# Reordering the first two batches of an attention-plus-MoE kernel, and unused matmuls in its pauses

## The chip, the cores and the metric

The kernel runs on one core of a Trainium2 chip. The core has a matrix engine (TensorE: PE in the profile, PEld for its weight loads), a vector engine (VectorE, DVE), a scalar engine (ScalarE, ACT), a general engine (GpSimd, POOL), and SyncE (SP), which here only issues DMAs. Each engine works through its own queue in order and waits on semaphores that the others raise. The metric is device microseconds of one execution; lower is better.

## What is computed

The attention takes 8 batches of 8 heads, 576 queries each, 64 numbers a head, and 16 extra "beacon" keys and values that every query may see. Its output, laid out as 4608 tokens of 512 numbers, goes through two matrices with a leaky ReLU between them.

```python
k_all = np.concatenate([beacon_k, k], axis=2)      # 16 + 576 keys
v_all = np.concatenate([beacon_v, v], axis=2)
scores = q @ k_all^T / 8                           # causal over the 576, beacons open
a = exp(scores - max); a /= sum(a)
attn = a @ v_all                                   # (8, 8, 576, 64)
x = attn.transpose(0, 2, 1, 3).reshape(4608, 512)
h = x @ w_in                                       # 512 -> 2048
out = max(0.01 * h, h) @ w_out                     # 2048 -> 512
```

## The kernel before

**Groups.** A group g is one batch and one pair of heads: 8 x 4 = 32 groups. The keys, beacons first, form five blocks of at most 128 (c = 0 to 4). Scores are computed with keys on the partitions and queries along the row, so the causal shape makes later blocks narrower. `score(g, n)`, n = 0 to 3, does the matmuls of one PSUM tile of two banks (L297), each as two matmuls on 64 partitions for the two heads, and the exponential into SBUF (L306, ACT). Two such PSUM tiles exist, so score n waits for the exponential n-2. `masks(g)` zeroes what a query may not see, with four affine_selects on POOL (L320). There are three buffers of probabilities, used in turn.

**From probabilities to x.** `value(g, half)` multiplies probabilities by values, which carry a column of ones so that the sums come along (L351: 12 matmuls in half 0, 18 in half 1), then takes reciprocals (L360) and scales (L361) on DVE. `x_transposes(g)` turns the result with five transposes (L373) and copies it to xT (L378). `finish(g)` does that and notes how many chunks of 512 tokens are ready for the two MoE matrices.

**MoE work as filling.** `fill()` emits one piece of MoE work: either `moe1` (four 128x512 matmuls, L387, and a Prelu on ACT, L394) or a quarter of `moe2` (four matmuls, L409; after the fourth quarter a copy by DVE, L418, and a store by SP). The total number of pieces is fixed. From group 8 on, what is left is spread over the steps of a group by the slots of the main loop; after the last group the rest is done in a row.

**Two ways of turning q and k.** For batches 0 and 1 (groups 0 to 7), `t_q(g, which)` turns them on TensorE: 18 transposes of 64x64 (L247) and a copy from PSUM (L250). For k a small copy of the turned beacon keys into kT comes first (L238). From batch 2 on the data are permuted on POOL (`permute`, L164), turned by DMA (`turn_pairs`, L262) and put in order on POOL (`in_order`, L275 and L277), one group ahead of its scores. kT has two buffers.

**Loads.** q and k of batches are loaded by POOL's queue, with a cast on the way (`load_qk`, L135, four DMAs for half a batch); the very first pair of heads comes uncast by SP's and ACT's queues (`load_first_pair`, L152) and is cast by DVE (q, L471) and ACT (k, L472). Values come by SP's queue (`load_v`, L210 to L215) and are cast by POOL (`cast_v`, L224, one instruction for each key block). The MoE weights come by POOL's queue (L109, L114), in groups 3 to 6. Before the first scores, 34 matmuls of the identity with itself are issued whose result nobody reads (`warm_up`, L444), and the beacon keys of batch 0 are turned (`beacon_transposes`, L186, with copies L191).

**Order.** The order of every queue is written out by hand: the order of the statements in the source is that of each engine's queue. In the loop over groups, `loads(g)` comes first (POOL and SP), then for g < 8 scores 0 and 1, `finish(g-3)`, the transposes for the next group, `value(g-2, 0)`, scores 2 and 3, `value(g-2, 1)`, and the masks. At g = 8 a block without scores finishes groups 5 to 7 with fills between and then does 22 fills, while POOL and the DMAs bring batch 2.

Of the kernel before, what the change touches and what calls it, by code (L numbers as in the profile page):

```python
# [8 lines left out]
FP32 = mybir.dt.float32  # L9
# [6 lines left out]
def kernel(  # L16
# [11 lines left out]
    nc = tc.nc  # L28
# [64 lines left out]
    def make_ones():  # L93
        for t in v_bufs:
            nc.gpsimd.memset(t[:, :, :, D : D + 1], 1.0)
# [83 lines left out]
            in_=bk_raw[:, b0:b1, None, :].to_broadcast([128, b1 - b0, 2, D]),  # L179
        )  # L180

    def beacon_transposes(b0, b1):

        ps = ps_one.tile([128, 1024], BF16, name="tp", tag="one")
        for b in range(b0, b1):
            nc.tensor.transpose(  # L186
                ps[:, b * 128 : (b + 1) * 128], bk[:, b].rearrange("p e d -> p (e d)"), ident
            )
        for par in range(2):
            ps_ = slice(par * 64, par * 64 + 64)  # L190
            nc.vector.tensor_copy(  # L191
                out=bkT[ps_, b0:b1].rearrange("p b h n -> p (b h) n"),
                in_=ps[ps_, b0 * 128 : b1 * 128].rearrange("p (x e n) -> p e x n", e=2, n=NB)[:, par],
            )
# [26 lines left out]
    def cast_v(b, eng, c0=0, c1=NKB):  # L221
        t, dst = v_raws[b], v_bufs[b % 2]
        for c in range(c0, c1):
            eng.tensor_copy(out=dst[0 : ROWS[c], c, :, 0:D], in_=t[0 : ROWS[c], c])  # L224
# [61 lines left out]
    def score(g, n):  # L286
        qT, kT = qk[g]
        if n == 0:
            probs[g] = a_bufs[g % 3]
        aT = probs[g]  # L290
        parts = SCORES[n]
        sc = ps_sc.tile([128, 2, 512], FP32, name="sc", tag="sc")
        c0 = parts[0][3]
        for c, q0, w, col in parts:
            for par in range(2):
                ps_ = slice(par * 64, par * 64 + 64)
                nc.tensor.matmul(  # L297
                    out=sc[:, par, col - c0 : col - c0 + w],
                    lhsT=kT[ps_, c * 128 : (c + 1) * 128],
                    rhs=qT[ps_, q0 : q0 + w],  # L300
                    start=True,
                    stop=True,
                    skip_group_check=True,
                )
        w = sum(p[2] for p in parts)
        nc.scalar.activation(  # L306
            out=aT[:, :, c0 : c0 + w], in_=sc[:, :, 0:w], func=AF.Exp, scale=0.125
        )

    def masks(g):  # L310

# [125 lines left out]
            turn[0] = 0  # L437
        return can1 or can2

    def warm_up(n):  # L440

        ps = ps_one.tile([128, 512], FP32, name="av", tag="one")
        for i in range(n):
            nc.tensor.matmul(out=ps[:, 0:128], lhsT=ident, rhs=ident, start=True, stop=True)  # L444

    NG = B * NPAIR

    def has(g):
        return 0 <= g < NG
# [10 lines left out]
    with order:  # L460
# [5 lines left out]
        load_v(0, after=first)  # L466
        load_v(1)
        make_pads()
        make_ones()
        cast_beacon_k(0, 1, nc.scalar.copy)  # L470
        nc.vector.tensor_copy(out=first_cast[0], in_=first_raw[0])  # L471
        nc.scalar.copy(out=first_cast[1], in_=first_raw[1])  # L472
        cast_beacon_k(1, B, nc.gpsimd.tensor_copy)
        cast_v(0, nc.gpsimd, 0, 1)
        load_qk(1, 0)
        cast_v(0, nc.gpsimd, 1, 3)
        warm_up(34)
        beacon_transposes(0, 1)
        t_q(0, 0)
        t_q(0, 1, nc.scalar.copy)  # L480

        def loads(g):
            b, hp = divmod(g, NPAIR)
            if g == 1:
                cast_v(0, nc.gpsimd, 3, 5)
            elif g == 2:
                load_qk(1, 1)
            elif g == 3:
                cast_v(1, nc.gpsimd, 0, 3)
                load_w_in(0)  # L490
            elif g == 4:
                cast_v(1, nc.gpsimd, 3, 5)
                load_w_in(1)
                load_w_in(2)
            elif g == 5:
                load_w_in(3)
                load_w_out(0)
                load_w_out(1)
            elif g == 6:
                load_w_out(2)  # L500
                load_w_out(3)
            elif g == 7:
                load_qk(2, 0)
            elif g >= 2 * NPAIR:
                if has(g + 1):
                    in_order(g + 1)
                if b < B - 1:
                    if hp == 0:
                        load_v(b + 1)
                        load_qk(b + 1, 0)  # L510
                    else:
                        if hp < 3:
                            for which in range(2):
                                permute(b + 1, hp - 1, which)
                        if hp == 1:
                            load_qk(b + 1, 1)
                        else:
                            turn_pairs(b + 1, hp - 2)
                    if hp == 3:
                        cast_v(b + 1, nc.gpsimd)  # L520
# [5 lines left out]
        def finish(g):  # L526

            x_transposes(g)
            ready[0] = chunks_with(g)
            if g % NPAIR == NPAIR - 1:  # L530
                turn[0] = 1


        for g in range(NG + 3):
# [3 lines left out]
            if g < 2 * NPAIR:  # L538

                score(g, 0)  # L540
                score(g, 1)
                if has(g - 3):
                    finish(g - 3)
                if g == 2:
                    beacon_transposes(1, B)
                if g + 1 < 2 * NPAIR:
                    t_q(g + 1, 0)
                    t_q(g + 1, 1, nc.scalar.copy if g in (4, 6) else nc.vector.tensor_copy)
                if g > 2:
                    value(g - 2, 0)  # L550
                if g == 7:
                    fill()
                score(g, 2)
                score(g, 3)
                if g == 2:
                    value(0, 0)
                if g >= 6:
                    fill()
                if has(g - 2):
                    value(g - 2, 1)  # L560
                masks(g)
                continue

            if g == 2 * NPAIR:

                load_qk(2, 1)
                for grp in range(2):
                    for which in range(2):
                        permute(2, grp, which)
                    turn_pairs(2, grp)  # L570
                load_v(2)
                in_order(g)
                cast_v(2, nc.gpsimd)
                finish(g - 3)
                value(g - 2, 0)
                fill()
                value(g - 2, 1)
                fill()
                finish(g - 2)
                value(g - 1, 0)  # L580
                fill()
                value(g - 1, 1)
                fill()
                fill()
                finish(g - 1)
                for n in range(22):
                    fill()
                loads(g)
# [70 lines left out]
```

The softmax here doesn't subtract the row's maximum and nothing guards it: scores larger than these inputs give would overflow.

## Time and profile before

| | |
|---|---|
| median of 6 runs | 356.26 us (355.72 to 356.88) |
| the profiled execution | 357.3 us, its span 355.6 us |
| mean granted TensorE clock | 0.966 |
| PE busy | 341.3 us, 96% of the span |
| POOL busy | 202.4 us, 57% |
| ACT busy | 189.2 us, 53% |
| DVE busy | 95.3 us, 27% |
| DMA | 40.87 MB, mean 115 GB/s |

The span runs from the first to the last instruction on the core. Lines of the page give busy tenths for 40 equal slices of the span (8.9 us each); `PEclk` is the clock that TensorE was granted, in tenths of full speed. Lines of the timeline read: start in us, length in us, engine, source line, operation, output<-inputs, shapes, number of instructions merged, and in brackets the engine's idle time before and what ended it. An issue of a DMA by POOL counts as busy time of POOL.

### The profile page before, as it was taken

How to read it: one execution, taken by the hardware profiler on the slowest of the kernel's cores; microseconds unless marked ns; L12 is line 12 of the kernel's file. 1: busy time of each engine (PE TensorE's matmuls, PEld its weight loads, DVE VectorE, ACT ScalarE, POOL GpSimd, SP SyncE). 2: the span in 40 equal slices, each digit the busy share in tenths (PEclk: the TensorE clock that was granted, in tenths of full speed). 3: DMA queues.
4: the chain of work that ended last, by engine and by line, in shares of the span. 5: the costliest groups of instructions: out<-in, count | busy, mean ns of one | idle time of the engine just before them, and what ended most of it. 6: DMA issues, size and time to landing. Idle time of an engine off the chain costs nothing.

```text
span 355.6 us, 7297 instructions
## 1 busy us (share of the span) xinstructions
PE 341.3 (96%) x2959; PEld 175.2 (49%) x3002; DVE 95.3 (27%) x231; ACT 189.2 (53%) x278; POOL 202.4 (57%) x343
## 2 busy tenths in 40 slices
PE   5899999999999999999999999999999999999996
PEld 5567554434444444444444544444444554444444
DVE  2396550001434213311232223222322241000111
ACT  3947945387454873378337843686348403733300
POOL 7599847489898899957695769574441100000000
PEclk9556999999999999999999999999999999999999
DMA  8999999998897996992579355900110011000012
GB/s 166 212 207 161 195 207 198 225 181 135 125 200 131 160 171 103 152 230 41 97 139 223 65 98 107 184 2 1 61 59 2 0 62 59 2 29 29 31 59 88
DMA packets 86929, 40.87 MB, mean 115 GB/s; under 512 B 69872, under 2 KB 82160, under 8 KB 86896
## 3 DMA queue, kind: packets, MB, share of 16 engines
q1 hardware_dynamic: 73456, 26.75, 35.4%
q0 software_dynamic: 13152, 13.34, 25.0%
q8 instruction: 23, 0.38, 0.4%
q10 hardware_dynamic: 288, 0.33, 0.4%
q14 instruction: 10, 0.08, 0.1%
HBM read 37.22 MB, written 9.44 MB: 131 GB/s over the span
## 4 chain that ended last, share of the span: by engine, by line
PE 91%; DVE 3%; ACT 2%; DMA 1%; issue 1%
PE acc L409 35%; PE acc L387 35%; PE sc L297 9%; PE av L351 9%; PE tp L373 2%; PE tp L247 1%; DMA v_raw<-in_k_dram 1%; DVE osb L418 1%; ACT aT L306 1%; DVE xT L378 1%; DVE kT L238 1%; ACT k_cast L472 0%; PE tp L186 0%; DVE qT L250 0%; DVE kT L250 0%
## 5 line engine op out<-in xcount | busy, mean ns | idle before, releaser
L387 PE MATMUL acc<-xT,w_in_sb 128*128 128x512 bf16 x554 | 138.4, 379 | 2.7 <-DVE xT L378 1.4
L306 ACT ACTIVATE aT<-sc 128x1024 bf16<-128x1024 f32 (+3 forms) x128 | 104.3, 870 | 65.2 <-PE sc L297 65.0
L409 PE MATMUL acc<-w_out_sb,gT 128*128 128x512 bf16 (+1 forms) x571 | 136.3, 373 | 1.5 <-issue 0.6
L394 ACT ACTIVATE gT<-acc 128x512 bf16<-128x512 f32 x144 | 85.9, 601 | 79.2 <-PE acc L387 79.2
L320 POOL TENSOR_SCALAR_AFFINE_SELECT aT<-aT 128x384 bf16<-128x384 bf16 (+2 forms) x128 | 52.9, 447 | 52.5 <-PE av L351 40.0
L409 PEld LDWEIGHTS <-gT 128*128 128x128 bf16 x592 | 53.3, 98 | 58.7 <-issue 6.1
L387 PEld LDWEIGHTS <-w_in_sb 128*128 128x128 bf16 x576 | 51.9, 98 | 59.5 <-issue 4.2
L418 DVE COPY osb<-acc 128x512 f32<-128x512 f32 (+1 forms) x37 | 25.0, 677 | 134.7 <-PE acc L409 134.6
L351 PEld LDWEIGHTS <-aT 128*128 128x128 bf16 (+1 forms) x960 | 38.9, 101 | 14.9 <-issue 3.3
L351 PE MATMUL av<-v_aug,aT 128*128 128x65 bf16 (+1 forms) x960 | 42.2, 199 | 0.1
L297 PE MATMUL sc<-qT,kT 64*128 64x80 bf16 (+4 forms) x384 | 38.2, 305 | 3.0 <-ACT aT L306 1.5
L361 DVE TENSOR_TENSOR x_nat<-av,rec 128x384 bf16<-128x384 f32 x64 | 31.4, 491 | 2.2
L224 POOL CAST v_aug<-v_raw 128x512 bf16<-128x512 f32 (+1 forms) x40 | 23.2, 620 | 8.9 <-DMA v_raw<-in_v_dram 8.9
L277 POOL COPY kT<-k_turn 128x576 bf16<-128x576 bf16 x24 | 28.1, 1170 | 0.0
L277 POOL COPY qT<-q_turn 128x576 bf16<-128x576 bf16 x24 | 28.1, 1169 | 0.0
L360 DVE RECIPROCAL rec<-av 128x6 f32<-128x6 f32 x64 | 11.9, 186 | 59.9 <-PE av L351 59.9
L378 DVE COPY xT<-tp 128x576 bf16<-128x576 bf16 x32 | 14.5, 454 | 48.2 <-PE tp L373 48.2
L297 PEld LDWEIGHTS <-kT 64*128 64x128 bf16 x384 | 13.0, 97 | 28.7 <-issue 18.8
L135 POOL DMA_DIRECT2D k_raw<-in_k_dram x31 | 19.3, 624 | 2.9 <-DMA w_out_sb<-in_moe_w_out_dram 2.9
L135 POOL DMA_DIRECT2D q_raw<-in_q_dram x31 | 19.0, 613 | 2.0 <-DMA w_out_sb<-in_moe_w_out_dram 1.9
L164 POOL COPY q_nat<-q_raw 128x1152 bf16<-128x1152 bf16 x12 | 13.7, 1145 | 6.1 <-DMA q_raw<-in_q_dram 6.1
L373 PEld LDWEIGHTS <-x_nat 128*128 128x128 bf16 (+2 forms) x160 | 11.4, 100 | 9.6 <-DVE x_nat L361 2.0
(36 smaller groups left out, 89.7 us busy)
## 6 DMA issues: line engine op xcount, KB each, us to landing
out_dram<-osb SPq DMA_DIRECT2D x35, 256.0 KB, 2.0
v_raw<-in_v_dram SPq DMA_DIRECT2D x24, 256.0 KB, 5.2
q_raw<-in_q_dram POOLq DMA_DIRECT2D x31, 144.0 KB, 5.0
k_raw<-in_k_dram POOLq DMA_DIRECT2D x31, 144.0 KB, 5.5
w_in_sb<-in_moe_w_in_dram POOLq DMA_DIRECT2D x4, 512.0 KB, 6.8
w_out_sb<-in_moe_w_out_dram POOLq DMA_DIRECT2D x4, 512.0 KB, 12.0
v_raw<-in_v_dram SPq DMA_DIRECT2D x8, 224.0 KB, 3.9
v_raw<-in_v_dram SPq DMA_DIRECT2D x8, 160.0 KB, 5.0
```

The source lines that it names most:

```text
L135: dma = nc.gpsimd.dma_start(out=dst[e * RP : (e + 1) * RP], in_=src[b, h0 : h0 + 2].rearrange("h (p i) d -> p h i d", i=RI),)
L224: eng.tensor_copy(out=dst[0 : ROWS[c], c, :, 0:D], in_=t[0 : ROWS[c], c])
L277: nc.gpsimd.tensor_copy(out=dst.rearrange("c (p i) -> c p i", i=RI), in_=t[:, :, e].rearrange("c i p -> c p i"),)
L297: nc.tensor.matmul(out=sc[:, par, col - c0 : col - c0 + w], lhsT=kT[ps_, c * 128 : (c + 1) * 128], rhs=qT[ps_, q0 : q0 + w], start=True, s ...
L306: nc.scalar.activation(out=aT[:, :, c0 : c0 + w], in_=sc[:, :, 0:w], func=AF.Exp, scale=0.125)
L320: nc.gpsimd.affine_select(out=part, in_=part, compare_op=ALU.is_ge, fill=0.0, base=base, channel_multiplier=-1, pattern=pattern,)
L351: nc.tensor.matmul(out=avv[:, n, 0 : D + 1], lhsT=aT[0 : ROWS[c], par, a0 : a0 + 128], rhs=va[0 : ROWS[c], c, 2 * hp + par, :], start=(c = ...
L361: nc.vector.tensor_tensor(out=x_nat[:, t0:t1].rearrange("p t e d -> p (t e) d"), in0=avv[:, :, 0:D], in1=rec[:, n0:n1, None].to_broadcast( ...
L387: nc.tensor.matmul(out=acc, lhsT=w_in_sb[:, j, fc * 128 : (fc + 1) * 128], rhs=xT[:, j, i * 512 : (i + 1) * 512], start=(j == 0), stop=(j ...
L394: nc.scalar.activation(out=gT[i][:, fc, :], in_=acc, func=AF.Prelu, alpha=0.01)
L409: nc.tensor.matmul(out=acc[:, 0:w], lhsT=gT[i][:, fc, t * 128 : (t + 1) * 128], rhs=w_out_sb[:, fc, c0 : c0 + w], start=(fc == 0), stop=(f ...
L418: nc.vector.tensor_copy(out=osb[:, 0:w], in_=acc[:, 0:w])
```

## The change

Eight parts, all in the first two batches or ahead of them:

1. First keys: the cast of the first pair's k is split by head between ACT and DVE.
2. `warm_up(34)` becomes `keep_busy(34)`; five more runs of unused matmuls are put in: 6 after the first beacon transposes, 6 and 10 after the two first `t_q`, 12 at the end of group 0 and 6 at the end of group 1. All write one PSUM tile.
3. The copies of the first beacon keys go from DVE to ACT.
4. `make_ones` moves behind the cast of the remaining beacon keys on POOL; the value casts of batch 0 are all issued ahead of the loop: two blocks before `load_qk(1, 0)`, three behind it. Before, it was one, then two, and two more in group 1.
5. The masks of group 0 are made by DVE, by multiplying with a triangle of ones (`make_tri` on POOL, `masks_by_tri`).
6. In groups 0 to 7 the order becomes: scores 0 and 1, transposes for the next group, scores 2 and 3, both halves of `value(g-2)`, `finish(g-3)`.
7. The fills of groups 6 and 7 beside scores 2 and 3 go; one fill is added at g = 8, before `finish(5)`. One piece less is done before the 22 fills, and so one more later.
8. The beacon transposes of the other batches move from group 2 to group 1.

```diff
-    def beacon_transposes(b0, b1):
+    def beacon_transposes(b0, b1, copy=nc.vector.tensor_copy):
...
-            nc.vector.tensor_copy(
+            copy(
                 out=bkT[ps_, b0:b1].rearrange("p b h n -> p (b h) n"),
...
+    tri = singles.tile([128, 128], BF16, name="tri")
+
+    def make_tri():
+
+        nc.gpsimd.memset(tri, 1.0)
+        nc.gpsimd.affine_select(
+            out=tri,
+            in_=tri,
+            compare_op=ALU.is_ge,
+            fill=0.0,
+            base=0,
+            channel_multiplier=-1,
+            pattern=[[1, 128]],
+        )
+
+    def masks_by_tri(g):
+
+        aT = probs[g]
+        diag = aT[:, :, 512 : 512 + 3 * 464].rearrange("p e (c x) -> p e c x", c=3)[:, :, :, 0:128]
+        for part, seen in (
+            (aT[:, :, 0:112], tri[:, None, NB:128].to_broadcast([128, 2, 112])),
+            (diag, tri[:, None, None, :].to_broadcast([128, 2, 3, 128])),
+            (aT[0:80, :, 1648:1728], tri[0:80, None, 0:80].to_broadcast([80, 2, 80])),
+        ):
+            nc.vector.tensor_tensor(out=part, in0=part, in1=seen, op=ALU.mult)
...
-    def warm_up(n):
-
-        ps = ps_one.tile([128, 512], FP32, name="av", tag="one")
+    busy = []
+
+    def keep_busy(n):
+
+        if not busy:
+            busy.append(ps_one.tile([128, 512], FP32, name="av", tag="one"))
         for i in range(n):
-            nc.tensor.matmul(out=ps[:, 0:128], lhsT=ident, rhs=ident, start=True, stop=True)
+            nc.tensor.matmul(out=busy[0][:, 0:128], lhsT=ident, rhs=ident, start=True, stop=True)
...
-        make_ones()
         cast_beacon_k(0, 1, nc.scalar.copy)
         nc.vector.tensor_copy(out=first_cast[0], in_=first_raw[0])
-        nc.scalar.copy(out=first_cast[1], in_=first_raw[1])
+        keep_busy(34)
+        beacon_transposes(0, 1, nc.scalar.copy)
+        nc.scalar.copy(out=first_cast[1][:, 0], in_=first_raw[1][:, 0])
+        nc.vector.tensor_copy(out=first_cast[1][:, 1], in_=first_raw[1][:, 1])
+        make_tri()
         cast_beacon_k(1, B, nc.gpsimd.tensor_copy)
-        cast_v(0, nc.gpsimd, 0, 1)
+        make_ones()
+        cast_v(0, nc.gpsimd, 0, 2)
         load_qk(1, 0)
-        cast_v(0, nc.gpsimd, 1, 3)
-        warm_up(34)
-        beacon_transposes(0, 1)
+        cast_v(0, nc.gpsimd, 2, 5)
+        keep_busy(6)
         t_q(0, 0)
+        keep_busy(6)
         t_q(0, 1, nc.scalar.copy)
+        keep_busy(10)
...
-            if g == 1:
-                cast_v(0, nc.gpsimd, 3, 5)
-            elif g == 2:
+            if g == 2:
                 load_qk(1, 1)
...
                 score(g, 0)
                 score(g, 1)
-                if has(g - 3):
-                    finish(g - 3)
-                if g == 2:
-                    beacon_transposes(1, B)
                 if g + 1 < 2 * NPAIR:
                     t_q(g + 1, 0)
                     t_q(g + 1, 1, nc.scalar.copy if g in (4, 6) else nc.vector.tensor_copy)
-                if g > 2:
+                score(g, 2)
+                score(g, 3)
+                if g == 1:
+                    beacon_transposes(1, B)
+                if g < 2:
+                    keep_busy((12, 6)[g])
+                if g >= 2:
                     value(g - 2, 0)
+                    value(g - 2, 1)
+                if g >= 3:
+                    finish(g - 3)
                 if g == 7:
                     fill()
-                score(g, 2)
-                score(g, 3)
-                if g == 2:
-                    value(0, 0)
-                if g >= 6:
-                    fill()
-                if has(g - 2):
-                    value(g - 2, 1)
+                if g == 0:
+                    masks_by_tri(g)
+                    continue
                 masks(g)
                 continue
...
                 in_order(g)
                 cast_v(2, nc.gpsimd)
+                fill()
                 finish(g - 3)
                 value(g - 2, 0)
```

## The prediction

> **What bounds the kernel now.** I read the page first, then the windows of TensorE, the timeline, and last the POOL timeline further on.
>
> ```profile
> PE   5899999999999999999999999999999999999996
> PEclk9556999999999999999999999999999999999999
> 5.80:9.22 3.42, 1.57 (x46) 1.00 1.24 214
> 26.28:29.70 3.42, 3.42 (x62) 0.50 0.96 148
> 29.70:33.11 3.41, 3.41 (x42) 0.50 1.11 151
> 33.11:36.52 3.41, 3.03 (x82) 1.00 1.24 206
> ...
> 26.28:29.70 3.42, 1.75 (x41) 0.50 0.96 148
> 33.11:36.52 3.41, 0.95 (x40) 1.00 1.24 206
> ```
>
> The first two lines are the page's: TensorE is full in nearly every slice, so the time falls only by what makes it reach its dense part sooner. The clock row shows the opening at half clock: by the finer windows from 9.22 to 33.11. Windows read: busy, instructions, clock, DMA share, GB/s; the last two lines count transposes alone. The clock changes every 3.41 us at most. Take transposes off: 5.80:9.22 had only 0.52 us of other matmuls (its transposes took 1.05) and full clock was lost; 33.11:36.52 had 2.08 (3.03 - 0.95) and kept it; 26.28:29.70 had 1.67 and did not raise it; 29.70:33.11 had 3.13 and did. So transposes seem not to count.
>
> ```profile
> 9.02 3.16 ACT L306 ACTIVATE aT<-sc 128x1024 bf16<-128x1024 f32 x4 [0.49 <-PE sc L297]
> 21.51 0.99 PE L297 MATMUL sc<-qT,kT 64*128 64x512 bf16 x4 [0.66 <-DVE kT L250]
> 26.71 1.00 PE L297 MATMUL sc<-qT,kT 64*128 64x512 bf16 x4
> 36.68 0.43 PE L373 MATMUL tp<-ident,x_nat 112*128 112x112 bf16 x5
> 37.04 0.47 PE L247 MATMUL tp<-ident,q_raw 64*64 64x64 bf16 x18
> 37.73 0.54 PE L351 MATMUL av<-v_aug,aT 128*128 128x65 bf16 x12
> 38.21 0.48 PE L297 MATMUL sc<-qT,kT 64*128 64x336 bf16 x8
> 39.49 0.72 PE L351 MATMUL av<-v_aug,aT 128*128 128x65 bf16 x18
> ```
>
> Groups 3 and 4 begin at 21.51 and 26.71: 5.20 us a group at half clock, TensorE without a pause. At full clock the pieces are (start to start) x transposes 0.36, q and k transposes 0.69, values 0.48 and 0.66; four exponentials take ACT 3.16 (3.27 later).
>
> **Part by part: the start.** The first keys' cast, 1.15 us on ACT from 6.18, is halved between ACT (0.6) and DVE (0.94/2): keys' transposes start at 6.85, not 7.38, and the first score follows 1.21 later as now (7.38 to 8.59): 8.1. The 10 unused matmuls (0.053 each at full clock, half the 0.107 of the warm-up's 34) lie under that copy, the first 6+6 under the wait for the casts. Beacon copies moved to ACT (0.38 from 5.1) lie before the keys land at 6.16.
>
> **Groups 0 to 2, if the clock holds.** Group 0: first exponential 0.47 after its first score, two exponentials 1.86, so score 3 can go at 2.38 and ends at 2.55; 12 unused matmuls 0.64: group 1 at 8.1+3.2=11.3. The masks of group 0 go to DVE: three tensor_tensor of 224, 768 and 160 elements a partition, which the trace doesn't show. Below, at the rate of the 576-element copy in 0.46 (L378), 1152 elements: 0.9 us; above, by L361 (384 in 0.56, 256 in 0.42, so 0.14 each and 1.1 ns an element): 1.7. I take 1.3, as near to one as to the other; they wait for the fourth exponential (8.1+0.43+3.16=11.7) and push qT, kT of group 2 (0.76+0.16+0.75) to 14.8. Group 2 starts then, TensorE itself being free at 14.7 (7 beacon transposes 0.4 and 6 unused 0.32 included). Its values need batch 0's last rows, which land at 18.15 by the landing events; cast 0.6: they end near 18.95, however fast the rest is. This wait of 1.3 us covers the uncertain masks.
>
> DVE against POOL: the 128x16 copy (L238) takes 0.16 alone but 1.98 at 18.83, while POOL's masks run to 20.77. So the new masks may meet POOL's two casts at 12.5 to 14.2, 0.6 each, +1.2 at most; the cover takes that. [...]
>
> **Groups 3 to 7.** New order: scores, transposes, scores, both value halves, x transposes. Score 3 still waits 2.38 for the second exponential, then 0.17+0.48+0.66+0.36: 4.05 a group. That beats 5.20, but loses to the old order at full clock: there 35.84 to 44.19, 8.35 us, held two groups and three fills (0.87 each, from L387 to L409 to L387 at 58.82 and 59.68), 2.9 a group net, since values and fills lay in the wait for exponentials. Start of group 3 at 19.0, five groups 20.25, one fill: 40.1; then 3.94 (44.19 to 48.13 now) and the added fill 0.87: value(7,0) at 44.9 against 48.13. It has done one fill less: TensorE is ahead by 3.2-0.87=2.4 us. The fills find their weights: the last quarter of w_out is first read near 64.0-3.2 and lands at 52.00.
>
> Moves on POOL's queue: load_qk(1,0), four issues, now stands behind the second value cast, whose rows land at 13.54, so issues start near 14.1 instead of 13.06 and land near 19.0 to 22.1 (17.91 to 21.08 now). Group 3's transposes want the first at 19.5, k at 19.8: 0.3 lost, 1.05 at most. make_ones (1.06) goes into POOL's idle 3.62 before 12.51; make_tri likewise, after six issues; without that cover the first value cast would be 1.06 late. SP keeps its order. Masks 0 leave POOL (1.63), but its casts then wait for the rows of 18.15, so masks 1 start at 18.8 (19.18 now). Masks 4 to 7 (third piece done after 1.3, all after 1.6) follow two, three, two and four issues (0.75, the last four 0.6) from 29.44 on: third pieces done at 32.2, 36.1, 39.2 and 43.2; values 4, 5 and 7 want them at 33.7, 37.8 and 44.9, so nothing waits. One of the four single PSUM banks stays with the unused matmuls until group 1; three are left for two transposes a group, each copied out within 0.76: nothing.
>
> **What takes part of it back.**
>
> ```profile
> 28.63 1.16 POOL L224 CAST v_aug<-v_raw 128x512 bf16<-128x512 f32 x2
> 29.74 1.51 POOL L109 DMA_DIRECT2D w_in_sb<-in_moe_w_in_dram  x2
> ...
> 101.99 1.20 POOL L277 COPY kT<-k_turn 128x576 bf16<-128x576 bf16 x1
> 104.18 0.59 PE L297 MATMUL sc<-qT,kT 64*128 64x512 bf16 x4
> ```
>
> Group 13's kT is ready on POOL at 103.19 and used at 104.18: 0.99 to spare (groups 10 to 15: 3.86, 2.64, 1.08, 0.99, 1.33, 1.25). From 70 to 140 POOL is 87 to 99% busy, waiting for its own loads. What sets its start is not TensorE: batch 1's last values land at 28.69, only then are they cast (28.63 to 29.79) and the weight loads issued (29.74), DMA share stays near 1.2 until w_out lands at 52.00, and each load of batch 2 waits for one of these. I let this move up 0.3 (POOL's queue just before it is 0.3 to 0.5 earlier; bounds -0.5 and +1.2, the thin DMA stretch at 31.5 to 32.5). A 0.97 us wait of POOL for exponentials at 76.14 goes too, but the next q_nat (79.72) has its rows only at 79.58, so 0.14 counts. TensorE can keep 0.99+0.14+0.3=1.4 of its 2.4 us; the rest becomes waits for kT in groups 11 to 13. After that slack is 8 us and TensorE bounds to the end.
>
> Sum on the profiled execution: span 355.6-1.4=354.2, with its 1.7 around the span 355.9 against its 357.3; that execution lies 1.04 over the median of 356.26, so 354.9 in the runs' terms.
>
> **Does the clock hold?** In the same currency the windows of the new kernel would hold: first, 6 and 10 unused (0.5, 0.7 with their tails) and two scores 0.59: 1.8; second 0.48+0.83+0.59=1.9; third 1.6; then 2.33 per 4.05, 2.0. Known: lost at 0.52, kept at 2.08. They are nearer to the upper row, so I take held. [...]
>
> **Rivals.**
> - POOL's chain moves up with TensorE, whole: 2.4 kept, 353.9. For it, the waits for DMA in that chain; against, DMA saturated to 52 us.
> - The pieces cancel: batch 1's loads land a microsecond late and POOL's start slips 0.5: 355.6 to 356.9, no change.
> - Slower: the clock falls at 12.63 for want of counted matmuls. Group 1 takes 4.4 (six unused 0.64 and beacons 0.93 now on the path), group 2 4.7, groups 3 and 4 5.2, group 5 4.2 with the clock back: group 6 at 35.0, group 8 at 44.0, value(7,0) at 48.8, 0.65 behind and a fill short: +1.5, 357.8. It decides from about two lost groups (1.15 each against 2.4). For it, windows under 2.08; against, 0.52 lies far below.
>
> **Numbers.** Forecast 0.50, first rival 0.14, no change 0.09, slower 0.27. Under 0.2% (0.7 us) this kernel's measurement can't be told from no change. Forecast's own range 353.7 to 355.7 (POOL's bounds); the whole 353.4 to 358.0, leaving out the ends of the first and last case. Faster 0.58 (a little of the forecast falls inside 0.2%), same 0.12, slower 0.30.
>
> **What would show it.** Right: granted clock 1.00 from about 6 us, mean above 0.99; group 3 near 19, group 8's first fill near 40; waits of L297 for POOL's kT in groups 11 to 13. Wrong: half clock between 9 and 30 (third rival), kT waits absent with value(7,0) near 45 (first), q or k transposes waiting for DMA in group 3 (second).

## The result and the profile after

The median after is 359.27 us (27 runs, 356.63 to 362.76), the kernel before on the same chip 356.61 (62 runs, 355.04 to 359.65). The ratio is 1.0068, 95% interval 1.0052 to 1.0085: slower by 0.68%, where 354.9 was forecast, a gain of 1.4 on the 356.26 that was known then. Ratios, here and below, leave out slow executions, those over 1.5% above the fastest of their kernel (three of these 27), so they can differ from the quotient of two medians. The profiled execution took 357.61 us; only four of the 27 were quicker, so it flatters the kernel by 1.7 us.

From the page of the kernel after: span, TensorE's and POOL's busy tenths, the clock, and the queue kind "instruction" (packets, MB, share).

```profile
span 355.9 us, 7381 instructions
PE   8797899999899999999999999999999999999995
POOL 7499927399799599987695769574431100000000
PEclk9969999999999999999999999999999999999999
q8 instruction: 24, 0.39, 0.5%
```

The clock row shows one low slice where the kernel before had three, and TensorE's row begins with 8 where it had 5; the 7s and 8s behind it are the same work at a higher clock (mean granted 0.990 against 0.966). By these rows the opening is better, and the time must have gone elsewhere.

Windows of the kernel after, cut at the clock's own steps, which its trace shows at 5.35, 19.00 and 25.83, four and two times 3.41 us apart (busy us and instructions of PE, PEld, DVE, ACT, POOL, then clock, DMA share, GB/s); the last two lines count transposes and their copies alone (PE, DVE, ACT).

```profile
12.18:15.59 3.41, 2.77 (x77) 2.04 (x72) 2.37 (x6) 3.16 (x5) 1.61 (x3) 1.00 1.12 197
15.59:19.00 3.41, 2.02 (x58) 1.53 (x52) 1.92 (x5) 2.71 (x4) 3.41 (x7) 1.00 0.99 201
19.00:22.42 3.42, 3.29 (x59) 1.97 (x57) 1.95 (x5) 1.86 (x2) 3.42 (x8) 0.50 1.20 212
...
12.18:15.59 3.41, 1.38 (x59) 2.27 (x4) 0.00 (x0) 1.00 1.12 197
15.59:19.00 3.41, 0.41 (x27) 1.49 (x2) 0.00 (x0) 1.00 0.99 201
```

The clock fell at 19.00, behind the window with the least work (2.02 us), and stayed at half to 25.83. TensorE's timeline tells why that window is thin, and what it cost:

```profile
18.22 0.37 PE L377 MATMUL av<-v_aug,aT 128*128 128x65 bf16 x7 [0.52 <-POOL v_aug L224]
18.78 1.04 PE L377 MATMUL av<-v_aug,aT 128*128 128x65 bf16 x15 [0.18 <-POOL v_aug L224]
19.75 0.99 PE L297 MATMUL sc<-qT,kT 64*128 64x512 bf16 x4
...
25.01 0.97 PE L297 MATMUL sc<-qT,kT 64*128 64x512 bf16 x4
```

The values of group 0 wait for POOL's casts of batch 0's last rows, as the forecast had it; group 3, at half clock, then takes 5.26 us (19.75 to 25.01). At full clock the groups step by 3.93 (scores of groups 5, 6 and 7 at 29.14, 33.07, 37.00). Even so group 8 starts at 68.59 against 71.00: 2.4 us, less the piece of MoE work still owed (0.87), a lead of 1.5.

Where the lead goes is in the chain of waits of the kernel after (start, length, what):

```profile
85.34 1.60 POOL aT L346 x4
87.08 1.10 POOL qT L277
88.18 1.10 POOL kT L277
89.33 0.58 PE sc L297 x4
```

Before, this stretch of the chain is TensorE alone. Now it goes through POOL's masks and copies; scores of groups 11, 12 and 13 start 0.06 us after their kT. Group 13 starts at 104.22, before at 104.18. So much was forecast, with a loss of 1.0 of 2.4. What was not forecast is that POOL's chain itself is later: kT of group 9 is ready at 73.87 (72.46 before), of group 13 at 104.16 (103.19). One place is plain in POOL's timelines, the casts of batch 2's values. First the kernel after:

```profile
65.86 0.62 POOL L224 CAST v_aug<-v_raw 128x512 bf16<-128x512 f32 x1 [3.71 <-DMA v_raw<-in_v_dram]
66.64 0.62 POOL L224 CAST v_aug<-v_raw 128x512 bf16<-128x512 f32 x1 [0.17 <-DMA v_raw<-in_v_dram]
69.23 0.62 POOL L224 CAST v_aug<-v_raw 128x512 bf16<-128x512 f32 x1 [1.97 <-DMA v_raw<-in_v_dram]
```

and the third of these casts in the kernel before:

```profile
67.71 0.62 POOL L224 CAST v_aug<-v_raw 128x512 bf16<-128x512 f32 x1 [0.57 <-DMA v_raw<-in_v_dram]
```

The third block of rows comes 1.4 us later behind the second. The DMA view of 65 to 70 us shows what else is on the DMA engines (busy tenths in 40 slices, then each queue: packets, MB, share). After:

```profile
DMA  9999999999999999999999966538999999999985
q1 hardware_dynamic: 3624, 1.12, 106.4%
q8 instruction: 1, 0.02, 1.2%
```

and before:

```profile
DMA  9998899999999999999999999999999999999999
q1 hardware_dynamic: 3964, 1.22, 116.1%
```

In the kernel after a 16 KB packet of the queue "instruction" (at 65.7 us) lies among these loads, and from 67.9 to 68.4 the DMA engines have a half-empty stretch. Before, the neighbouring packets came at 53.1 and 76.7. This became the main theory.

### The profile page after: what moved, and what is told of

Its sections match the earlier page's. It is cut to its first block, busy times and chain, and to the rows that moved or that the text cites. A ratio compares the mean times of both kernels' runs of the same rounds, so it can differ in the third digit from the quotient of the medians.

```text
span 355.9 us, 7381 instructions
## 1 busy us (share of the span) xinstructions
PE 338.7 (95%) x2999; PEld 174.5 (49%) x3042; DVE 94.1 (26%) x233; ACT 188.7 (53%) x280; POOL 201.0 (56%) x341
## 4 chain that ended last, share of the span: by engine, by line
PE 86%; DMA 5%; POOL 2%; DVE 2%; issue 2%; ACT 1%; SPq 0%; ACTq 0%
PE acc L435 34%; PE acc L413 34%; PE av L377 8%; PE sc L297 8%; DMA v_raw<-in_v_dram 2%; PE tp L399 2%; DMA k_raw<-in_k_dram 2%; DMA v_raw<-in_k_dram 1%; ACT aT L306 1%; DVE osb L444 1%; DVE xT L404 1%; POOL kT L277 1%; PE tp L247 1%; POOL q_raw L135 0%; POOL aT L346 0%
## 5 line engine op out<-in xcount | busy, mean ns | idle before, releaser
L346 POOL TENSOR_SCALAR_AFFINE_SELECT aT<-aT 128x224 bf16<-128x224 bf16 (+1 forms) x124 | 50.8, 450 | 46.9 <-PE av L377 37.1
L377 PEld LDWEIGHTS <-aT 128*128 128x128 bf16 (+1 forms) x960 | 37.5, 99 | 15.4 <-issue 3.9
L297 PE MATMUL sc<-qT,kT 64*128 64x80 bf16 (+4 forms) x384 | 36.7, 290 | 6.9 <-ACT aT L306 5.3
L377 PE MATMUL av<-v_aug,aT 128*128 128x65 bf16 (+1 forms) x960 | 40.5, 196 | 0.9 <-POOL v_aug L224 0.7
L386 DVE RECIPROCAL rec<-av 128x6 f32<-128x6 f32 x64 | 11.9, 187 | 62.4 <-PE av L377 62.4
L399 PEld LDWEIGHTS <-x_nat 128*128 128x128 bf16 (+2 forms) x160 | 11.4, 99 | 6.4
```

The costliest lines, as they stand in the source:

```text
L297: nc.tensor.matmul(out=sc[:, par, col - c0 : col - c0 + w], lhsT=kT[ps_, c * 128 : (c + 1) * 128], rhs=qT[ps_, q0 : q0 + w], start=True, s ...
L346: nc.gpsimd.affine_select(out=part, in_=part, compare_op=ALU.is_ge, fill=0.0, base=base, channel_multiplier=-1, pattern=pattern,)
L377: nc.tensor.matmul(out=avv[:, n, 0 : D + 1], lhsT=aT[0 : ROWS[c], par, a0 : a0 + 128], rhs=va[0 : ROWS[c], c, 2 * hp + par, :], start=(c = ...
```

## The experiments

All were timed in five rounds beside the kernel before on the same chip (its medians there: 356.78 for e1 to e4, 356.65 for e5 to e8, 356.53 for e9 to e12, 356.78 for e13 to e16, 357.19 for e17 and e18). Ratios are to that kernel, with 95% intervals.

### Does POOL's chain set the end?

**e1: the kernel after, again.**

> The changed kernel itself, for a second execution under the profiler and for its scatter (27 runs so far from 356.63 to 362.76, against 355.04 to 359.65 before). Theory A: TensorE is ahead in the opening (value of group 7 starts near 45 to 46, 48.13 before) but meets kT of groups 9 to 13 late, as POOL's chain of casts, loads and orderings for batches 2 and 3 sets it; a slow execution then shows long waits of L297 for POOL's kT, and a late kT(9) (over 74), with the opening unchanged. Median 358.5 to 360. Rival B: in slow executions the clock falls in the opening: value of group 7 at 48 or later, mean clock 0.98 or less, no long waits for kT.

360.01 (1.0085, 1.006 to 1.011), its profile at 358.14. It shows the same: half clock from 18.85 to 25.68, waits for kT at groups 11 to 13, the third value block 1.98 late behind the second, the packet at 65.5.

**e2 and e3: the value casts of batch 2 moved behind the copies of group 9 and the loads after them**, in the kernel after and in the kernel before.

```diff
                 in_order(g)
-                cast_v(2, nc.gpsimd)
...
                 loads(g)
+                cast_v(2, nc.gpsimd)
```

> The changed kernel with one move on POOL: the five value casts of batch 2 stand behind in_order(9) and load_qk(3,0) instead of ahead of them. Theory A: kT(9) is ready by 66 instead of 73.87, kT(10) to kT(13) follow earlier, the waits for kT go, and TensorE keeps its lead of 1.5 to 2.4 us over the kernel before: 354.2 to 355.2, with a scatter no larger than that of before. Rival B (the opening is what is slow and varies): unchanged, 358.5 to 360.

> The kernel before with the same move of the five value casts. Theory A: its kT stands ready 0.99 us or more ahead, so the move is worth nothing there: 356.3 to 356.9. If the move is worth something by itself (a kernel before that now and then waits for kT): 355.5 to 356.2. Rival B: no change either.

e2: 357.88 (1.0027, 1.0006 to 1.0048). e3: 355.17 (0.9969, 0.9942 to 0.9997), quicker than both kernels. One reordering on POOL is worth some 1.5 to 2 us after (against the first timing and e1) and 1.1 to 1.6 before (by ratio and by median): the kernel before is itself near its chain's limit. Neither run met a band: e2 missed the 354.2 to 355.2 of theory A, and in its profile kT of group 9 was ready 11.4 us ahead while group 12 still waited for its own (ready at 99.71). The wait had moved, not gone.

**e5 and e6: the copies of groups 9 to 11 from POOL to DVE**, after and before.

```diff
-        first = nc.gpsimd.tensor_copy(out=kT[:, 0:NB], in_=bkT[:, b, hp])
+        copy = nc.vector.tensor_copy if 9 <= g <= 11 else nc.gpsimd.tensor_copy
+        first = copy(out=kT[:, 0:NB], in_=bkT[:, b, hp])
```

> The kernel after, with the key copies of groups 9 to 11 (about 3 us of work for each group on POOL) moved to VectorE. Theory A (the end is set by the chain of POOL and its transfers that makes kT of groups 9 to 13, and the lead of the opening is given back there): the waits of scores 11 to 13 for kT shrink or go, and the time is 354 to 355.5. Rival B (the opening itself is slower in the executions that are not profiled): the kT waits go and the time stays at 358 or above.

> The same move of the copies of groups 9 to 11 made to the kernel before. Theory A (both kernels stand against the same chain): 355.5 or below, a gain of about 1; the difference to the kernel after with the same move is then what the opening alone is worth, in theory 1 to 2.5 in favour of the new opening. Rival B: no gain here, about 356.6, and below the kernel after with the same move.

e5: 358.28 (1.0062, 1.0032 to 1.0091); e6: 355.93 (0.9977, 0.9958 to 0.9996). e6 gained 0.7; e5 gained 0.2 by the ratio and 1.0 by the median, which is not clear of noise. Both missed the bands of theory A. The profile of e5 says why: groups 9 to 11 have 5.5 to 9.5 us of slack, yet group 12 waits, its kT ready at 98.41 because the turned keys of batch 3's second half only land at 98.12. The chain is not POOL's work alone but loads, permuting, turning and copies in a row.

What decides the end shows in all twenty profiles. Time of the profiled execution, start of the scores of group 13, and the difference:

```
kernel   us      group 13   rest      kernel   us      group 13   rest
before   357.30  104.18     253.1     e9       355.84  102.45     253.4
after    357.61  104.22     253.4     e10      358.46  105.05     253.4
e1       358.14  104.75     253.4     e11      357.54  104.42     253.1
e2       359.89  106.49     253.4     e12      360.71  107.59     253.1
e3       354.39  101.27     253.1     e13      360.89  107.43     253.5
e4       356.86  103.44     253.4     e14      360.84  107.42     253.4
e5       358.43  105.21     253.2     e15      359.30  105.87     253.4
e6       357.21  103.89     253.3     e16      355.32  101.90     253.4
e7       358.95  105.54     253.4     e17      355.86  102.47     253.4
e8       359.81  106.32     253.5     e18      356.46  103.31     253.2
```

Over 6.3 us of spread in group 13, the rest varies by 0.4. The time is decided when group 13 begins, and in all but the kernel before, e3, e10, e12, e17 and e18 that is 0.06 us after its kT. For the kernel after a median of 359.27 thus means group 13 at about 105.9 (an estimate from these rows: no execution of it that slow was profiled).

### Is it the opening's order or its loads?

**e7: `load_qk(1, 0)` behind one value cast again. e8: the order of before in groups 3 to 7 and at g = 8**, only the first three groups in the new order.

```diff
-        cast_v(0, nc.gpsimd, 0, 2)
+        cast_v(0, nc.gpsimd, 0, 1)
         load_qk(1, 0)
-        cast_v(0, nc.gpsimd, 2, 5)
+        cast_v(0, nc.gpsimd, 1, 5)
```

> The kernel after, with the loads of the second batch's first half issued behind one cast of a value row again and not behind two. Theory A2 (the late start of that load pushes the chain of loads and POOL some 1 us later through groups 1 to 9): issue near 13 to 14, kT of groups 9 to 13 some 1 us earlier and the time 357.5 to 358.3. Rivals: no change against the kernel after, 358.5 to 360.

> The kernel after, with the order of before in groups 3 to 7 and at the start of the second stage (finish, next transposes, half of the values, scores, fills in groups 6 and 7, other half); only the first three groups keep the new order. Theory A: TensorE reaches group 8 with or without more lead and the kT waits take it, 358.5 to 360. Rival D (the new order in groups 3 to 7 is what costs): 356 to 357.

e7: 359.81 (1.0092, 1.0062 to 1.0122); e8: 359.51 (1.0086, 1.0057 to 1.0115). Neither helped, and e7 missed theory A2's band. The profile of e7 is the most telling of all: the clock held through the whole opening, group 8 began at 66.71, 4.3 us ahead of before, kT of group 9 was ready at 72.70, and the execution was still 1.7 us slower than the one of before. Its waits in TensorE's timeline:

```profile
88.84 0.89 PE L297 MATMUL sc<-qT,kT 64*128 64x512 bf16 x4 [2.17 <-POOL kT L277]
98.81 0.39 PE L297 MATMUL sc<-qT,kT 64*128 64x512 bf16 x2 [0.78 <-POOL kT L277]
```

and the window behind the first of them:

```profile
89.00:92.40 3.40, 3.40 (x15) 1.37 (x12) 0.33 (x1) 2.46 (x3) 0.00 (x0) 0.50 2.08 132
```

TensorE arrived early, stood 2.17 us for kT of group 11, and lost the clock for a window in its dense part. The same happened in e8 (wait of 1.95) and e10 (2.04). In e10 that window, and not kT, then set the end: kT of group 13 was ready 1.38 us before its use. So a lead that runs into a wait can cost more than it brought. It does not always: e4 waited 2.14 us and e13 2.42 and 2.88, and both kept the clock. Their waits lie across the step between two windows, which had 1.84 us of work or more each; those of e7, e8 and e10 lie within one, which was left with 1.2 to 1.5.

**e4: the kernel after with the first 34 unused matmuls only.**

```diff
-        keep_busy(6)
...
-                if g < 2:
-                    keep_busy((12, 6)[g])
```

> The changed kernel with only the first 34 unused matmuls; the 40 others are left out. Theory A: the clock falls near 9 us as before, TensorE loses its lead (value of group 7 near 48.8, mean clock near 0.96 to 0.97), the waits for kT shrink and the end is at 357.5 to 359.5. Rival C (the unused matmuls do not hold the clock, or only cost): 356 to 359.3 with the clock as in the changed kernel.

357.52 (1.0025, 1.0005 to 1.0046): without the other 40 the kernel is quicker by some 1.5 to 1.75 us, though its clock was at half from 9.54 to 19.78. Theory A had TensorE lose its lead here; it did not, and group 8 started at 66.75. The packet came at 72.0 and the third value block was 0.68 behind. This run could not tell whether the 40 cost by work, by the clock, or by their number.

### The number of matmuls, and where the packets fall

The packets are 16 KB each and begin near the same count of TensorE's instructions: in the twenty profiles at about the 1,700th of its weight loads and matmuls counted together (1,691 to 1,754) for the one near 62 to 77 us, and at the 1,948th to 2,026th for the next. 24 packets (0.39 MB) stand against 3,042 weight loads and 2,999 matmuls after, 23 against 3,002 and 2,959 before: one for each 250 to 260 instructions. That they carry TensorE's instructions is inferred from this count and from the queue's name; no run shows what is in them.

That a packet stretches the transfers it meets can be seen where nothing else disturbs them. Late in every profile the 256 KB stores of the output stand alone. Of those with no other transfer of the program in flight, the 263 without a packet took 1.66 to 2.03 us from issue to landing; the 24 with a packet that began from 0.2 us before the issue to 0.8 us behind it took 2.24 to 3.68. In 8 more the packet began 1.5 us or more behind the issue, and they took 1.97 to 2.13. Two neighbours of the kernel after, first 248 to 253 us, with the packet at 249.0:

```profile
DMA  0000000070027999810101000000000000000000
q8 instruction: 1, 0.02, 1.8%
out_dram<-osb SPq DMA_DIRECT2D x1, 256.0 KB, 3.3
```

and 253 to 258 us, without one:

```profile
DMA  0000000028999910000000000000000000000000
out_dram<-osb SPq DMA_DIRECT2D x2, 256.0 KB, 2.0
```

Nothing in the kernel waits for these stores. What remains to be shown is that packets on loads of the chain set the time.

**e9 and e10: the same columns in fewer, wider matmuls**, for the first 34 (e9: 9 instead of 34; the condition reads n == 34) or for the other 40 (e10: 12 instead of 40).

```diff
-        for i in range(n):
-            nc.tensor.matmul(out=busy[0][:, 0:128], lhsT=ident, rhs=ident, start=True, stop=True)
+        wide = n < 34
+        for i in range(0, n, 4 if wide else 1):
+            m = min(4, n - i) if wide else 1
+            nc.tensor.matmul(
+                out=busy[0][:, 0 : m * 128].rearrange("p (m c) -> p m c", m=m),
+                lhsT=ident,
+                rhs=ident[:, None, :].to_broadcast([128, m, 128]),
+                start=True,
+                stop=True,
+            )
```

> The kernel after, with the first 34 unused matmuls of 128 columns made as 9 of up to 512 columns: the same columns, 25 matmuls fewer, nothing else. Theory F: TensorE's instructions are fetched by 16 KB packets (queue kind 'instruction', some 256 instructions apart); the 40 added matmuls have moved these packets from 76.7 us (before) to 65.5 to 65.7 (after and its repeat), into the loads of the third batch's values, whose third block lands 2.0 us behind the second there and 0.6 in the kernel before. With 50 instructions fewer the packet comes at about 70, the block on time, kT of group 9 near 73.0, and the time is about 357.5. Rival G (the unused matmuls cost by the work or the clock): no change, 359 to 360.

> The kernel after, with the other 40 unused matmuls made as 12 wide ones: the same columns, 28 matmuls fewer. Theory F: as with the other 34, packet near 70, time about 357.5. Rival G: no change, 359 to 360.

e9: 357.62 (1.0023, 1.0002 to 1.0043), packet at 68.9. e10: 357.26 (1.0028, 1.0005 to 1.0051), packet at 70.7. Both intervals lie below that of the kernel after (from 1.0052). Two different sets of matmuls, with the same columns, gave 1.4 to 2 us (by ratios and by medians) when 25 and 28 were saved. The profiled executions are not typical of this: e10's, at 358.46, is slower than the one of the kernel after, e9's faster than its median by 1.8. The third value block of e10:

```profile
68.63 0.62 POOL L224 CAST v_aug<-v_raw 128x512 bf16<-128x512 f32 x1 [0.58 <-DMA v_raw<-in_v_dram]
```

**e11: the kernel before with the 40 unused matmuls.**

> The kernel before, with the 40 unused matmuls of 128 columns in the opening (6 before the first query transposes, 6 and 10 behind them, 12 and 6 in groups 0 and 1). Theory F: the packet of 76.7 moves to some 68, into the same loads, kT of group 9 about 1 us later, and the time goes up by 1 or more, to 357.5 to 359, although the clock in the opening is held better. Rival G2 (only the clock counts): group 8 starts earlier and the time falls to 355 to 356.

357.86 (1.0054, 1.0026 to 1.0081): slower by 1.3 (1.9 by the ratio), with the clock at 1.00 from 4.7 to the end of the dense part. Group 8 began at 66.91 instead of 71.00, and group 13 at 104.42 instead of 104.18. The packet came even earlier than expected, at 62.4, as TensorE itself was ahead; it lay on the turning transfers, the last of which landed 6.4 us behind the loads that they wait for (5.3 before). The third value block was on time (0.68 behind), so the time came out as theory F had it, but not by the block that it named.

**e13: e10 with the 28 matmuls put back, 8 columns wide.**

```diff
+        for i in range(n - -(-n // 4) if wide else 0):
+            nc.tensor.matmul(
+                out=busy[0][:, 0:8], lhsT=ident, rhs=ident[:, 0:8], start=True, stop=True
+            )
```

> The kernel after with its 40 unused matmuls made as 12 wide ones (the earlier run e10), and 28 more unused matmuls of 8 columns at the same five places, so that the number of matmuls is that of the kernel after again. Theory F (where the packets of TensorE's instructions fall): the packet comes back from 70.7 to about 65.5 and the time to 359 or above. Rival G (the work of the unused matmuls, or the clock): unchanged against the wide version, 357 to 357.7.

359.01 (1.0062, 1.0036 to 1.0089): 1.75 above e10's median and in theory F's band. By the ratios the difference is 0.34%, some 1.2 us, and the two intervals overlap, so this return is not clear of noise. The clock of the profiled execution held to the end of its dense part. The packets moved to 63.4 and 85.8; the third value block was on time again (0.58 behind), and the second packet lies on the loads of batch 3's second half, a place that was found afterwards. POOL's wait for them, first e13:

```profile
94.55 1.15 POOL L164 COPY q_nat<-q_raw 128x1152 bf16<-128x1152 bf16 x1 [4.36 <-DMA q_raw<-in_q_dram]
```

and e10, where the packet came at 91.1, as they were landing:

```profile
90.77 1.15 POOL L164 COPY q_nat<-q_raw 128x1152 bf16<-128x1152 bf16 x1 [1.57 <-DMA q_raw<-in_q_dram]
```

From issue to the last landing these loads took 11.2 us in e13 (83.9 to 95.1) and 8.3 in e10 (82.9 to 91.2); 10.5 in e7 and e8 with packets at 85.7 and 85.5, 9.4 and 9.5 in the kernel after and e1 (89.8, 90.4), 8.4 in e4 (90.9). With no packet among them it was 9.4 before, 10.1 in e6 and 9.8 in e14, so packets are not the only thing that stretches them.

### What does not explain it

**e14: TensorE held back by 14 unused matmuls of 512 columns ahead of group 8, on e10.**

```diff
                 for n in range(22):
                     fill()
+                busy.clear()
+                keep_busy(28)
+                keep_busy(28)
                 loads(g)
```

> The kernel after with its 40 unused matmuls made as 12 wide ones, and 14 more unused matmuls of 512 columns (some 3 us at full clock) behind the 22 fills, ahead of the scores of group 8. Theory H (TensorE's lead makes the chain later, because the writes of the output come 3 us earlier and lie on the loads of the last batch that is in the chain): kT of groups 12 and 13 comes earlier and the time falls to 356 to 356.8. Theory A alone (the chain does not see the lead): kT as before, the time unchanged at 357 to 357.7, as the lead of some 4 us is lost at kT anyway. Rival E (TensorE sets the end): 360.

359.16 (1.0056, 1.0035 to 1.0077), none of the three. Holding TensorE back did not make the chain earlier, which speaks against theory H. The size stays open (the interval overlaps that of e10): the profiled execution had lost the clock from 18.29 to 28.53, and its loads were already 2 us late at 31 us, ahead of the edit; its packets came at 72.7 and 95.2, the latter just ahead of the turning of batch 3's second half, whose first transfer took 3.2 us, as in the kernel after (3.5).

**e12: the last loads of values moved.** Its edit also left the casts of the values of batches 3 to 6 out, so it does not compute the same output and POOL has 20 casts less to do.

> The kernel after, with the loads of the last batch's values issued behind its second pair of transposing DMAs and cast behind the copies of group 13, not issued beside the loads of its first half of q and k. Theory A (the end is set by the chain of loads and POOL that makes kT of groups 9 to 13): that half lands 2 to 3 us sooner, kT of groups 11 to 13 comes 3 to 5 us sooner, TensorE's lead is kept and the time is 353.5 to 356. Rival: 358.5 or above.

357.88 (1.004, 1.0014 to 1.0066), not 353.5 to 356. The half of q and k that should have landed 2 to 3 us sooner took 7.0 us instead of 7.6. This speaks against the loads of values as what held it; with the casts gone too it is no clean test.

### Is the new opening worth anything without that chain?

**e15: e10 and e2 together. e16: e15 with the load order of e7.**

> The kernel after with its 40 unused matmuls made as 12 wide ones, and the value casts of the third batch behind the copies of group 9 and the loads that follow them. Theory A with F: the two gains add up (2.7 from the count, 2.1 to 2.5 from the casts), 354.5 to 356. Rival: both took away the same wait, 357 to 358.

> As the run before it, with the loads of the second batch's first half behind one value cast and not two. Theory A2 (an earlier stream of loads moves the chain by as much): 0.3 to 1 below that run. Rival: the same as that run.

e15: 356.60 (0.9996, 0.9967 to 1.0024); e16: 356.05 (0.9983, 0.996 to 1.0007). The first missed its band by 0.6, so the gains add up only in part; the second came 0.55 below it, as expected of A2, but well within the noise, and the same edit alone (e7) had gained nothing.

**e17 and e18: the loads of each later batch's second half issued ahead of the next copies**, on e16 (new opening) and on e3 (old opening).

```diff
+                if b < B - 1 and hp == 1:
+                    load_qk(b + 1, 1)
                 if has(g + 1):
                     in_order(g + 1)
...
-                        if hp == 1:
-                            load_qk(b + 1, 1)
-                        else:
+                        if hp > 1:
                             turn_pairs(b + 1, hp - 2)
```

> The run e16 (new opening, 40 unused matmuls as 12 wide ones, third batch's value casts late, second batch's first load behind one cast), with the loads of each later batch's second half issued ahead of the copies of the next group instead of behind those and two more copies: about 4.5 us earlier for the last batch that is in the chain. Theory A: the wait of POOL for these loads goes, kT of group 12 comes 1 to 3 us earlier, TensorE's lead is kept, 353.7 to 355.3. Rival: another wait of POOL takes its place (kT of group 10 comes 2.4 us later and holds TensorE at group 10), 355.5 to 357.

> The run e3 (old opening, third batch's value casts late), with the same move of the loads. Theory A: TensorE itself sets the end there, as kT of groups 12 and 13 was only 0.3 to 0.4 ahead of it: no more than 0.5 gained, 354.6 to 355.4, so that the new opening comes out 0 to 1.5 below the old one. Rival: as e17, 355.5 to 357.

e17: 356.03 (0.9974, 0.995 to 0.9998); e18: 356.42 (0.996, 0.9935 to 0.9984). Both missed the bands of theory A and lie in those of their rivals. Both beat both kernels, e3 still has the lowest median (e18 the lowest ratio), and the two openings cannot be told apart. In the profiles kT of groups 12 and 13 is now ahead of its use, by 2.6 us in e17 and 3.1 in e18, so the old wait is gone; group 8 starts at 66.55 with the new opening and at 70.13 with the old, 3.6 us apart. Of this 0.9 is the piece of MoE work still owed, and 1.9 is lost at group 10, as the rival had it. TensorE's waits for kT in e17, 66 to 106 us (sum, times, longest):

```profile
PE sc L297 <- POOL kT L277: 1.8, 1, 1.8
```

At group 13 the two stand at 102.47 and 103.31, 0.8 apart. The opening is faster by itself, and no version here could keep more of it.

## Why the prediction was wrong, step by step

- **The start and groups 0 to 2** were right: first score 7.96 (8.1), group 1 at 11.30 (11.3), group 2 at 14.71 (14.8). Group 3 came 0.75 late, at 19.75 (19.0). The new masks took 0.97 us on DVE, below the 1.3 taken. They ended at 12.29, ahead of POOL's cast at 12.52, so the two did not meet, and the 1.2 us allowed for that was not needed.
- **"The clock holds"** fell in the profiled execution. The window of 15.59 to 19.00 was counted at 2.0 us without transposes and had 1.61, because TensorE's wait for batch 0's last rows, priced as a delay of group 3, was not taken out of the window. The currency was wrong too: with transposes subtracted the clock was kept at 1.39 (12.18 to 15.59) and lost at 1.61. The price was 1.3 us in group 3. But it is not the cause of the result: the profiled executions of e7 and e13 held the clock throughout the opening and took 358.95 and 360.89. And of the 27 executions of the kernel after, the eight with a granted clock of 0.994 or more have a median of 360.5 us, the other 19 of 359.1.
- **The step of a group**, 4.05, was near: 3.93 at full clock. The lead of 2.4 came to 1.5 in this execution, and some 3.4 (4.3 less the piece owed) where the clock held.
- **The waits for kT in groups 11 to 13** came where they were named.
- **"I let this move up 0.3"** is the step that failed, and where the sign was lost. POOL's chain had bounds of 0.5 later and 1.2 earlier; in the profiled execution it came 1.0 later (104.16 against 103.19 for group 13's kT), and for the median of 359.27 it is estimated some 2.6 later (105.8). Part of this had been priced at nothing: the added matmuls, since they "lie under" waits of TensorE. As work they do. But with their number the packets of the queue "instruction" moved (from 76.7 us to 65.7). That the number of matmuls costs is shown: e9 and e10, with the same columns in fewer matmuls, gain 1.4 to 2 us, and the 40 added to the kernel before cost 1.3 to 1.9 (e11). That packets stretch transfers is shown by the stores (2.24 to 3.68 us against at most 2.03). That they do it on the loads of the chain, and that this is how the number costs, is argued from single profiles: the third value block agrees in the kernel after and in e1, not in e11 and e13. The forecast's lower end, 353.7, counts the 0.3 twice; by its own sum it is 354.0.
- **The second rival** ("POOL's start slips") had the right place with a smaller size. The third, the clock, named the right danger and the wrong reason for slower.
- **What stays open:** e4, e9 and e10 are still 0.23 to 0.28% above the kernel before, some 0.8 to 1 us, with the packets elsewhere. In three profiles of the new opening with the clock at half to 28.5 us or later (e12, e14, e15) the loads of batch 1's second half landed at 30.6 to 31.1 us instead of 28.9 (e10), so POOL's masks and the loads queued behind them may carry that on; with half clock to some 26 us it was 29.2 to 29.6 (the kernel after, e1, e2) and 30.6 (e5). This was seen, not tested.

## What to carry to other kernels

Find the wait that ends last after the stage that is changed, and price the change on that chain too; a lead that ends in a wait is worth nothing, and here a wait of 2.17 us that fell within one window of the clock took the clock with it (e7). Unused instructions were not free here though they lay under waits (40 less gave 1.5 to 1.75 us in e4, 28 less with the same columns 1.4 to 2 in e10): count what they move, the packets of the queue "instruction" among it, and prefer few wide ones. When a kernel gets slower against the argument, make the suspected piece the same work in another number of instructions, and put the number back without the work.

## What was not expected of the hardware

- A single 16 KB packet of the queue "instruction" stretched the transfers it met: lone 256 KB stores took 2.24 to 3.68 us with one beginning near their issue (24 stores) and at most 2.03 without (263). How one packet of 0.88 to 1.62 us (the 24 of the kernel after) does this is not shown. Between two value blocks there were 1.97 and 1.98 us with the packet at 65.7 and 65.5, 0.57 to 0.68 without (before, e4, e10); but gaps of 1.7 to 2.3 us stand without a packet in e3 and e15 to e18 too, where loads of batch 3 run beside.
- In the openings of all twenty profiles (windows of 3.41 us, transposes included) the clock was lost behind every window with TensorE busy 2.03 us or less, nine of them, and kept behind every one with 2.25 or more; between, it went both ways (lost at 2.23, kept at 2.05). With transposes subtracted the order is lost: kept at 1.26, lost at 2.03. Later windows lie lower: up to 105 us five with 1.78 to 1.98 kept the clock, and three with 1.2 to 1.5 lost it. For raising it transposes did not seem to count in these openings: windows with up to 3.42 us busy, but 1.83 or less without transposes, never raised it; between 1.9 and 2.5 it went both ways. To lose it, 1.4 us without work in one window was enough (15.59 to 19.00 after), and so was a wait of 2.17 us within one (e7), while 2.88 us across two were not (e13).
